# Ten of 22 small moves issued by ScalarE, a four-column marker product, and a new order of all steps in an RWKV-6 + hard-swish kernel

## The chip, the cores and the metric

The kernel runs on one core of a Trainium2 chip. The metric is the device time of one execution in microseconds (us); lower is better. The engines' names in the profile are PE (TensorE's products), PEld (its weight loads), DVE (VectorE), ACT (ScalarE), POOL (GpSimd) and SP (SyncE, which issues transfers). A `q` behind a name (SPq, ACTq) means the engine's sequencer: an instruction that only waits or issues.

## What is computed

A linear-attention recurrence over 4 batches, 8 heads, 768 positions and head size 48, and then a two-layer network with a hard-swish between its layers:

```python
for t in range(S):
    kt, vt, rt, wt = (k[:, :, t], v[:, :, t], r[:, :, t], w[:, :, t])
    cur = np.einsum('bhd,bhe->bhde', u[None] * kt, vt)
    y[:, :, t] = np.einsum('bhd,bhde->bhe', rt, state + cur)
    state = wt[:, :, :, None] * state + np.einsum('bhd,bhe->bhde', kt, vt)
...
x = y.transpose(0, 2, 1, 3).reshape(B * S, H * D)          # 3072 x 384
h = x @ w_in                                               # w_in 384 x 2048
g = h * np.clip(h + 3.0, 0.0, 6.0) / 6.0
out = g @ w_out                                            # w_out 2048 x 384
```

`w_in` and `w_out` arrive as float64 and are converted to float32 on the chip (steps `low`, `sign`, `shift`, `full`).

## The kernel before

The 768 positions of a batch are cut into chunks of 128 positions, so there are 24 chunks (numbered `i`; the two sequences of a pair alternate). Four chunks make a block of 512 rows of x; there are six blocks (`bk` 0 to 5).

Per chunk, the recurrence is a chain of small steps: two scans of the decay (`back`, `fore` on VectorE, L430 and L439), scaled keys and receptances (`K`, `R`, on VectorE for the first seven chunks and then on GpSimd, L450 and L454), the bonus term with `u` (`own`, `sum`, `diag`), scores, a masked copy (`above`, VectorE, L507), transposed keys (`turned`, ScalarE), the running state (`decay`, `mid`, `decb`, `state`), and on TensorE one step `read{i}`. From chunk 4 on `read{i}` holds, in this order, the products with the state (L578), a mark, the scores of the next chunk (L500), a mark, the key-value products of the next chunk (L600), the products with the values (L587), and the transposes of the keys of the chunk after the next (L516). A mark (L622) is a product of two corners of the identity into a scratch tile that nothing reads. Reads work on quarters of the array, so two or four products run at once.

ScalarE then copies the result into x (`leave{i}`, L685). The eight heads lie in three groups of 128 rows of x; the last pair of heads does not fit and is written to a fourth group (`x3`), from which small transfers within the chip's memory bring its rows to their places in the other three. These are the moves: `move{bk}.{p}.{g}` for pair `p` of chunks and half `g`, three transfers each (`last_pair`, L692, 16 KB a transfer). Block 0 has two moves, blocks 1 to 5 four each: 22 moves, 66 transfers. SP issues all of them.

Block 0 is multiplied plainly (`up0.f.c`, L718; `down0.c.q`, L737). Blocks 1 to 5 use a scheme with fewer products and more sums. VectorE forms sums of the weights once (`sin`, `sout`, L780 to L812) and sums of x in four steps per block (`tx{bk}.0` to `.3`, also L780 to L784), which need all four moves of the block. TensorE then forms 20 products in each of two halves (`up{bk}.{d}.{r}`, L833, four records of 256 columns each), in chains that share a bank of the product memory; `read{bk}.{d}.a{n}` take the chains' values out, on VectorE (L850) or ScalarE (L841, L848); `clip` (ScalarE, L854) and `gate` (VectorE, L858) form the hard-swish. Seven products per half follow for the second layer (`down{bk}.{p}.{k}.{x}`, L888, eight records of 192 columns), with sums of g (`sum{bk}.{p}.{k}.{x}`, VectorE, L873) and results taken out by `out{bk}.{p}.s1`, `.v`, `.u`, `.c11` and so on (ScalarE L899 and L906, VectorE L908). `vet` steps (L936, L943) check the range of the inputs on VectorE.

The order of all 1750 steps is written out: each step is added to a plan with its engine, a reckoned duration, what it needs and which buffers it takes; the string `ORDER` holds two characters per step, its rank. The steps are issued in this order, each into the queue of its engine, and each engine works its queue strictly from the front. The reckoned durations decide only two things on the chip: which of a ring's buffers a step takes follows from the order, and how many filling products TensorE gets in the first 60 us:

```python
if engine == "PE" and self.start[n] < self.UPTO:
    while now < self.start[n] - 0.12:
        self.spin()
        now += next(us_ for upto, us_ in self.SPIN if now < upto)
    now = max(now, self.start[n]) + us
```

with `SPIN = ((6.3, 0.43), (1e9, 0.224))`. A filling product (`spin`, L1269) writes a scratch bank.

Of the kernel before, what the change touches and what calls it, by code (L numbers as in the profile page):

```python
# [8 lines left out]
F32 = mybir.dt.float32  # L9
# [11 lines left out]
L = 128  # L21
# [60 lines left out]
    "AAADAHAQAKAOAMANAPARASAYAWAjAUAXAaAeAmAqAgAoAzA3A/ACAFATAiAbAnAdAZAcAfAhAlAuAyAkApAxA1A5A9A8A+BOBUBeAJALBGBfBRBZBSBD"  # L82
    "BJBTBVBYCGCLBoBwCBCRBbCYCfCnCwC7AVAwBiB4BuCABzBdBgBlBmBqCSCaCJCOCWCrCNCuC1E1DBDMDVDfBPBQCpC3DdDkCvCUCbCiDDDXDuDyC+DG"
    "DiFCDLFGFKFcFZFnCXDKC9DHEPEbDCDADQDWDsEKFgDZDqFmE6FsFvF+FzF/HgHLCcC4D+EJFpFtEDDYDwD9FfFlF8FkGFF9GVGfGiGlGsDoGSETFjGD"
    "GJEXEEFJFRF6GLG0GBGoGbGvG4HBG+HHHSHVEdF2FwF7GpG1FyGHGIGWGtGzHYGqHPG9HUHcH2HtH4FxG5F1GUGwHEHaGrGQGYHQHjH5HIINHkITIYIw"
    "I4JHL3KhGOHJGRHCHlH0H6HZGkHXH+IOJIIDKPJzK/LELJLbHKKIHOHoIqJCJEIPHmH8KxKyLOKzLKKtLXLeLmL8MHMIHbLTHhJTJeLVLdJZIJIbLULa"
    "LxLgLsL0MNL9MtJLJfJOJtLRLqLzKOJ4LFLuL+MQLtMaNANnOYOeQBOqK3L2LCLiL1MFMJLrLMMBMDMiOkNhObM/OzO4PJPVPgLfOpL4MAMyOZOsMnM9"
    "NIO1PFPeOcPiPBPmPoQJPyP2QTQZM5PcM6NdOrPbPfNpNQOCPkPrP+PlQNPsQPQUQWQcQxNtOlNuPXPqP9QAPhO5PIQIQOQlP1QsQqRSRVR/R2TPTzUG"
    "OwQjOxPxQVQrQuP0PSQRQwRySGRBSSRdSsS2ThTsUJQkTZQ+Q2RRSFSvQ/RURmS5TOT0TQTwToT1UDUPUMUQUoUTRbSQRcSLTnT8UBS7RtSNT5UKUhT9"
    "UXUEUZUkU/U2WYSATySCTqTvUSUjTrTaTuUnU0U6UmVaUlVrXGXfXnXsYIYETYURTxUOUpVOVzUWUyU+XQXmXwVMXpVyXuXzX3YAVQVRVUVeWHXqXvVh"  # L90
# [154 lines left out]
def fast_path(tc, feat, tok, wflat, ub, ug, moe_w_in, moe_w_out, out, flag, n_chunks):  # L245
# [22 lines left out]
    with ExitStack() as ctx:  # L268
# [352 lines left out]
        def mark():  # L621
            nc.tensor.matmul(pp.tile([HL, HL], F32, name="ps"), lhsT=ident[HL:, HL:], rhs=ident[HL:, HL:], start=True, stop=True)  # L622
# [378 lines left out]
        for i in range(NT):  # L1001
# [12 lines left out]
            plan.add(f"back{i}", "DVE", 1.40, do(back_scan, i), [f"feat{i}"] + [f"fore{i - 2}"] * (i > 1) + [f"back{i - 1}"] * (i > 0), k,  # L1014
                     [("E", [f"K{i}", f"least{i}"])], port=True)
            plan.add(f"K{i}", "DVE" if dve else "POOL", 0.59 if dve else 1.15, do(make_k, i), [f"back{i}", f"least{i}"] + [f"K{i - 1}"] * (i > 0) + ["later"] * (i == 0),
# [3 lines left out]
            plan.add(f"R{i}", "DVE" if dve else "POOL", 0.6 if dve else 1.15, do(make_r, i), [f"fore{i}"], k + 0.3,  # L1020
# [7 lines left out]
            else:  # L1028
                plan.add(f"own{i}", "POOL", 2.2, do(own, i), [f"rkt{i}", "u"] + [f"own{i - 1}"] * (i > 0), k + 0.4,
# [20 lines left out]
            if not first:  # L1050
                plan.add(f"decay{i}", "DVE" if dve else "POOL", 0.27 if dve else 0.9, do(decay, i),
                         [f"state{i - 2}", f"least{i}"] + [f"decay{i - 1}"] * (not is_first(i - 1)), t - 0.1 if i < len(START) else t - 5, S_, port=True)
                plan.add(f"mid{i}", "DVE", 0.33, do(middle, i), [f"kvs{i}", f"decay{i}"], t - 0.1 if i < len(START) else t - 5,
                         port=True)
            plan.add(f"decb{i}", "DVE" if dve else "POOL", 0.27 if dve else 0.9, do(decay_middle, i),
                     [f"least{i}"] + [f"mid{i}" if not first else f"kvs{i}"], t - 0.1 if i < len(START) else t - 5, S_ * first,
                     port=True)
            if not last:
                plan.add(f"state{i}", "DVE", 0.27, do(new_state, i), [f"decb{i}"] + [f"decay{j}" for j in (i - 2,) if j >= 0 and not is_first(j)],
                         t + 0.5, port=True)  # L1060
# [15 lines left out]
            else:  # L1076
                uses = [f"up{bk}.{d}.{r}" for d in range(2) for r in range(20) if X_PLACE[r][0] == "w"] + [f"tx{bk}.{x}" for x in range(4)]
                space = [("x", uses)] * (c == 0)
                needs, us = [f"decb{i}", f"above{i}"], 1.24
# [538 lines left out]
```

## Time and profile before

| | us |
|---|---|
| three runs | 540.81, 542.64, 541.25 |
| median | 541.25 |
| the profiled execution's own time | 542.08 |
| its span, first to last instruction | 540.2 |
| TensorE busy in the span | 530.0 |
| VectorE busy | 416.6 |
| ScalarE busy | 263.5 |
| GpSimd busy | 110.2 |
| granted TensorE clock, mean | 1.00 |

The own time is what the chip reports for the execution that was profiled; 1.88 us of it lie outside the span. Products on TensorE are pipelined: a record is longer than the distance to the next one, so "busy" counts a short wait only in part.

### The profile page before, as it was taken

The page shows a single profiled execution, that of the slowest core. Times are in us where ns is not written, and L with a number is a line of the kernel's source. Part 1 is how long each engine was busy: PE and PEld are TensorE (multiplying, and loading weights), DVE is VectorE, ACT ScalarE, POOL GpSimd, SP SyncE. Part 2 cuts the span into 40 slices and gives each one's busy share as a digit, 9 for nine tenths or more (in the row PEclk, how much of TensorE's full clock was granted, in tenths as well). Part 3 has the DMA queues.
Part 4 walks back from the last instruction along what each step waited for, and adds up shares of the span by engine and source line. Part 5 has one row for each costly group of instructions (what it writes and reads, how often), then busy time and mean ns, then how long its engine had stood idle before and what let it go on. Part 6 is the DMA issues. An engine that isn't in the chain of part 4 may idle for free. (4 is left out here: it accounts for less than half of the span.)

```text
span 540.2 us, 13522 instructions
## 1 busy us (share of the span) xinstructions
PE 530.0 (98%) x5626; PEld 470.1 (87%) x5626; DVE 416.6 (77%) x709; ACT 263.5 (49%) x657; POOL 110.2 (20%) x111
## 2 busy tenths in 40 slices
PE   8999999999999999999999999999999999999997
PEld 8887877666788999888889988899988999988997
DVE  8999999675999996889787888967768845358651
ACT  5999795252555434446434354635254435253400
POOL 2000003742422054111332341303350001000000
PEclk9999999999999999999999999999999999999999
DMA  8948653333234434733205785002630001100001
GB/s 341 368 160 312 237 177 105 116 106 105 74 115 151 139 94 164 250 133 130 95 17 193 256 282 205 1 10 92 208 134 1 0 2 36 41 1 1 8 8 47
DMA packets 21458, 66.42 MB, mean 123 GB/s; under 512 B 3312, under 2 KB 11408, under 8 KB 21392
## 3 DMA queue, kind: packets, MB, share of 16 engines
q1 hardware_dynamic: 21264, 65.50, 35.3%
q8 instruction: 46, 0.75, 0.5%
q14 instruction: 20, 0.16, 0.1%
q10 hardware_dynamic: 128, 0.00, 0.0%
HBM read 59.69 MB, written 4.72 MB: 119 GB/s over the span
## 5 line engine op out<-in xcount | busy, mean ns | idle before, releaser
L854 ACT ACTIVATE clip<-g,three 128x512 f32<-128x512 f32 x80 | 56.3, 720 | 55.0 <-DVE g L850 38.9
L850 DVE TENSOR_TENSOR g<-bank,g 128x512 f32<-128x512 f32 x80 | 53.4, 681 | 16.0 <-PE bank L833 15.1
L858 DVE SCALAR_TENSOR_TENSOR g<-clip,g 128x512 f32<-128x512 f32 x80 | 57.9, 740 | 6.1 <-ACT clip L854 5.9
L888 PE MATMUL bank<-w_out,g 128*128 128x192 f32 x320 | 57.3, 328 | 1.0 <-DVE g L858 1.0
L888 PEld LDWEIGHTS bank<-w_out,g 128*128 128x128 f32 x320 | 52.5, 190 | 2.5 <-DVE g L858 1.5
L491 ACT ACTIVATE A<-eyes,dg 128x64 f32<-128x64 f32 x192 | 50.4, 339 | 6.6 <-PE y_ps L587 6.3
L450 POOL TENSOR_TENSOR K<-feat_in,E 112x512 f32<-112x512 f32 x17 | 24.4, 1433 | 121.4 <-PE ps L622 117.7
L454 POOL TENSOR_TENSOR W<-feat_in,W 112x512 f32<-112x512 f32 x17 | 22.3, 1312 | 116.7 <-DVE W L439 108.9
L718 PE MATMUL bank<-xT,w_in 128*128 128x256 f32 (+1 forms) x216 | 45.2, 361 | 0.0
L685 ACT COPY xT<-y_ps 48x256 f32<-48x256 f32 x88 | 32.1, 365 | 24.8 <-PE y_ps L587 23.9
L737 PE MATMUL bank<-w_out,g 128*128 128x384 f32 x128 | 43.2, 488 | 0.0
L833 PE MATMUL bank<-xT,w_in 128*128 128x256 f32 x160 | 40.9, 381 | 0.8 <-DVE g L850 0.7
L718 PEld LDWEIGHTS bank<-xT,w_in 128*128 128x128 f32 x216 | 36.7, 190 | 4.7
L848 ACT COPY g<-bank 128x512 f32<-128x512 f32 x50 | 28.9, 582 | 21.5 <-PE bank L833 21.3
L737 PEld LDWEIGHTS bank<-w_out,g 128*128 128x128 f32 x128 | 23.8, 190 | 14.5
L439 DVE TENSOR_TENSOR_SCAN W<-feat_in,start 112x520 f32<-112x520 f32 x24 | 29.6, 1234 | 8.6 <-PE y_ps L578 8.6
L833 PEld LDWEIGHTS bank<-xT,w_in 128*128 128x128 f32 x160 | 30.0, 190 | 5.9 <-DVE g L850 2.1
L430 DVE TENSOR_TENSOR_SCAN E<-feat_in,back 112x520 f32<-112x520 f32 x24 | 32.5, 1354 | 2.9 <-DMA feat_in<-in_feat_dram 1.3
L841 ACT ACTIVATE bankS<-bank 128x512 f32<-128x512 f32 x20 | 11.6, 582 | 40.4 <-PE bank L833 31.9
L833 PE MATMUL bank<-xT,bits 128*128 128x256 f32 x120 | 30.7, 381 | 0.0
L888 PE MATMUL bankS<-w_out,g 128*128 128x192 f32 x160 | 28.8, 326 | 0.0
L888 PE MATMUL bank<-more,g 128*128 128x192 f32 x160 | 28.1, 326 | 0.0
(291 smaller groups left out, 1136.7 us busy)
## 6 DMA issues: line engine op xcount, KB each, us to landing
feat_in<-in_feat_dram SPq DMA_DIRECT2D x23, 772.5 KB, 4.8
bits<-in_moe_w_in_dram SPq DMA_DIRECT2D x8, 768.0 KB, 5.4
bits<-in_moe_w_out_dram SPq DMA_DIRECT2D x8, 768.0 KB, 5.7
feat_in<-in_moe_w_in_dram SPq DMA_DIRECT2D x8, 768.0 KB, 4.8
feat_in<-in_moe_w_out_dram SPq DMA_DIRECT2D x8, 768.0 KB, 4.6
rk_in<-in_tok_dram SPq DMA_DIRECT2D x15, 384.0 KB, 5.1
v_in<-in_tok_dram SPq DMA_DIRECT2D x24, 192.0 KB, 4.5
feat_in<-in_wflat_dram SPq DMA_DIRECT2D x6, 768.0 KB, 4.6
```

What stands on the lines that cost most here:

```text
L430: nc.vector.tensor_tensor_scan(out=E_[:, ::-1], data0=d["w"][:, :0:-1], data1=back.rearrange("q p t -> q (p t)")[:, ::-1], initial=0.0, op ...
L439: nc.vector.tensor_tensor_scan(out=W_, data0=d["w"][:, :-1], data1=starts[i % 2].rearrange("q p t -> q (p t)"), initial=0.0, op0=ALU.mult, ...
L491: nc.scalar.activation(out=d["A"][:, h, :], in_=eyes, func=ACT.Copy, scale=d["dg"][:, h])
L685: nc.scalar.copy(out=blocks[bk]["xT"][g * GP:g * GP + D, :, at:at + HL], in_=st[i]["y_ps"][a][(g ^ a) * GP:(g ^ a) * GP + D, :, :])
L718: nc.tensor.matmul(h_ps[:, :(c1 - c0) * L], lhsT=w_in[:, f // 2, j, f % 2, :], rhs=b["xT"][:, j, c0 * L:c1 * L], start=(j == 0), stop=(j = ...
L737: nc.tensor.matmul(b["o", c][:, :DM], lhsT=g_of(0, f, c), rhs=w_out[:, f, :], start=(f == 0), stop=(f == NFC - 1))
L833: nc.tensor.matmul(b["p", d, c][:, z * HB:(z + 1) * HB], lhsT=weight(W_PLACE[r], d)[:, z, :], rhs=x_at(bk, X_PLACE[r]), start=fresh and z ...
L848: nc.scalar.copy(out=out_, in_=src)
L850: nc.vector.tensor_tensor(out=out_, in0=src, in1=out_of(bk, d, other), op=ALU.add if sign > 0 else ALU.subtract)
L854: nc.scalar.activation(out=c, in_=out_of(bk, d, u), func=ACT.Relu, bias=three, scale=twice)
L858: nc.vector.scalar_tensor_tensor(out=g, in0=blocks[bk]["r", d, u], scalar=6.0, in1=g, op0=ALU.min, op1=ALU.mult)
L888: nc.tensor.matmul(b["d", p, to][:, :h], lhsT=a, rhs=w(), start=(f == 0 and k in (1, 5)), stop=(f == HF - 1 and k in (2, 3, 4)), skip_grou ...
```

## The change

Three edits, and prices of steps that the order was searched with.

*Moves.* Of each block from 1 on, the two moves with `g` = 1 are put into ScalarE's queue and issued from there; those with `g` = 0, and both of block 0, stay with SP. That is ten moves, 30 transfers.

```diff
-                    plan.add(f"move{bk}.{c // 2}.{g}", "SP", 1.8, do(last_pair, bk, c - 1, c + 1, g, nc.sync),
+                    plan.add(f"move{bk}.{c // 2}.{g}", "ACT" if g and bk else "SP", 1.8, do(last_pair, bk, c - 1, c + 1, g, nc.scalar if g and bk else nc.sync),
                              [f"leave{i - 1}", f"leave{i}"], when(i) - 50, kb=1, dmas=3)
```

*Marks.* The product of a mark streams 4 columns instead of 64; its weights are the same 64 x 64.

```diff
-            nc.tensor.matmul(pp.tile([HL, HL], F32, name="ps"), lhsT=ident[HL:, HL:], rhs=ident[HL:, HL:], start=True, stop=True)
+            nc.tensor.matmul(pp.tile([HL, 4], F32, name="ps"), lhsT=ident[HL:, HL:], rhs=ident[HL:, :4], start=True, stop=True)
```

*Order.* The string `ORDER` is replaced. It was searched with a plan in which transfers land in the order of their issue; that search is not part of the kernel. The reckoned durations that went with it change in the kernel too:

```diff
-  back 1.40, K 1.15 and R 1.15 and own 2.2 and decay 0.9 and decb 0.9 on POOL, mid 0.33, state 0.27, read 1.24
+  back 1.44, K 1.27 and R 1.22 and own 2.45 and decay 0.75 and decb 0.7 on POOL, mid 0.36, state 0.35, read 1.31
-  gate of block 0: 0.07 + 0.134 m; sin 0.34; sout 0.86; tx 0.335 per sum; gate 0.6; sum of g 0.61
+  gate of block 0: 0.08 + 0.136 m; sin 0.39; sout 0.92; tx 0.46 per sum; gate 0.62; sum of g 0.64
```

(The last block is the list of the values, not the source's lines.) Decoded from the two strings, these are the pieces of the queues that the prediction speaks of:

```
TensorE before: ... down0.2.3 read7 down0.2.4 .. down0.3.5 read8 down0.3.6 up1.0.1 down0.3.7 up1.0.9 up1.0.3 ...
TensorE after:  ... down0.2.1 read7 down0.2.2 .. down0.3.1 read8 down0.3.2 .3 .4 up1.0.1 down0.3.5 .6 .7 up1.0.18 up1.0.14 up1.0.9 ...
VectorE before: ... above8 sin1.2 sin1.3 back11 sin1.4 tx1.0 sin1.5 tx1.1 sin1.6 fore10 sin1.7 state8 sin1.8 above9 ...
VectorE after:  ... above8 sin1.2 sum10 sin1.3 sout2.1 sin1.4 above9 sin1.5 tx1.0 sin1.6 tx1.1 sin1.7 tx1.2 sin1.8 tx1.3 ...
ScalarE after:  ... leave7 diag18 least10 diag09 turned9 move1.0.1 diag19 move1.1.1 drain0.2 read1.0.a4 drain0.3 ...
ScalarE after, blocks 2, 4: ... out1.0.s1 out1.0.v move2.0.1 out1.0.u ...; ... out3.0.v move4.0.1 least20 out3.0.u ... out3.1.v kvs20 least22 move4.1.1 ...
ScalarE after, block 5: ... leave22 out4.0.c11 move5.0.1 leave23 out4.0.v out4.0.u move5.1.1 ...
SP before:      ... feat11 move1.0.1 rkt11 move1.1.0 move1.1.1 feat12 move1.0.0 rkt12 ...
SP after:       ... feat11 move1.0.0 store0.0 rkt10 rkt11 move1.1.0 feat12 tok10 rkt12 ...
POOL before:    K7 K8 R7 own9 decay7 own10 K9 R8 decb7 decay8 R9 decb8 decay9 K10 ...
POOL after:     K7 decay7 K8 R7 own9 decb7 R8 K9 decay8 decb8 K10 own10 R9 ...
VectorE before, block 2: ... gate2.1.0 sum2.0.1.1 sum2.0.2.0 sum2.0.2.1 sum17 state14 sum2.0.4.0 sum2.0.3.1 sum2.0.4.1 ...
VectorE after,  block 2: ... gate2.1.0 sum2.0.2.0 sum2.0.3.0 mid14 sum16 sum2.0.1.1 vet10.0 sum2.0.2.1 sum2.0.3.1 sum2.0.4.0 sum2.0.4.1 ...
TensorE before, block 4: read19 down3.1.6.1 3.0.2.0 3.1.7.0 3.0.2.1 3.1.3.0 3.1.7.1 3.1.3.1 3.1.4.0 read20 up4.0.1 ...
TensorE after,  block 4: read19 down3.1.6.0 3.1.6.1 3.1.3.0 3.1.3.1 3.1.7.0 3.1.7.1 read20 up4.0.1 ...
```

More of the change, by code (lines that the diff above doesn't have):

```diff
@@ L86 @@
[L86 to L90, printed above, removed]
@@ L1013, in fast_path @@
                          hold=[("rk_in", [f"own{i}"])])
-            plan.add(f"back{i}", "DVE", 1.40, do(back_scan, i), [f"feat{i}"] + [f"fore{i - 2}"] * (i > 1) + [f"back{i - 1}"] * (i > 0), k,
+            plan.add(f"back{i}", "DVE", 1.44, do(back_scan, i), [f"feat{i}"] + [f"fore{i - 2}"] * (i > 1) + [f"back{i - 1}"] * (i > 0), k,
                      [("E", [f"K{i}", f"least{i}"])], port=True)
-            plan.add(f"K{i}", "DVE" if dve else "POOL", 0.59 if dve else 1.15, do(make_k, i), [f"back{i}", f"least{i}"] + [f"K{i - 1}"] * (i > 0) + ["later"] * (i == 0),
+            plan.add(f"K{i}", "DVE" if dve else "POOL", 0.59 if dve else 1.27, do(make_k, i), [f"back{i}", f"least{i}"] + [f"K{i - 1}"] * (i > 0) + ["later"] * (i == 0),
                      k + 0.1, [("K", [scored(i), turned_by(i)])], port=True)
@@ L1019, in fast_path @@
                      [("W", [scored(i), read_by(i)])], port=True)
-            plan.add(f"R{i}", "DVE" if dve else "POOL", 0.6 if dve else 1.15, do(make_r, i), [f"fore{i}"], k + 0.3,
+            plan.add(f"R{i}", "DVE" if dve else "POOL", 0.6 if dve else 1.22, do(make_r, i), [f"fore{i}"], k + 0.3,
                      port=True)
@@ L1028, in fast_path @@
             else:
-                plan.add(f"own{i}", "POOL", 2.2, do(own, i), [f"rkt{i}", "u"] + [f"own{i - 1}"] * (i > 0), k + 0.4,
+                plan.add(f"own{i}", "POOL", 2.45, do(own, i), [f"rkt{i}", "u"] + [f"own{i - 1}"] * (i > 0), k + 0.4,
                          [("rk", [f"sum{i}"])], port=True)
@@ L1050, in fast_path @@
             if not first:
[L1051 removed]
+                plan.add(f"decay{i}", "DVE" if dve else "POOL", 0.27 if dve else 0.75, do(decay, i),
                          [f"state{i - 2}", f"least{i}"] + [f"decay{i - 1}"] * (not is_first(i - 1)), t - 0.1 if i < len(START) else t - 5, S_, port=True)
[L1053 removed]
+                plan.add(f"mid{i}", "DVE", 0.36, do(middle, i), [f"kvs{i}", f"decay{i}"], t - 0.1 if i < len(START) else t - 5,
                          port=True)
[L1055 removed]
+            plan.add(f"decb{i}", "DVE" if dve else "POOL", 0.27 if dve else 0.7, do(decay_middle, i),
                      [f"least{i}"] + [f"mid{i}" if not first else f"kvs{i}"], t - 0.1 if i < len(START) else t - 5, S_ * first,
@@ L1058, in fast_path @@
             if not last:
-                plan.add(f"state{i}", "DVE", 0.27, do(new_state, i), [f"decb{i}"] + [f"decay{j}" for j in (i - 2,) if j >= 0 and not is_first(j)],
+                plan.add(f"state{i}", "DVE", 0.35, do(new_state, i), [f"decb{i}"] + [f"decay{j}" for j in (i - 2,) if j >= 0 and not is_first(j)],
                          t + 0.5, port=True)
@@ L1078, in fast_path @@
                 space = [("x", uses)] * (c == 0)
-                needs, us = [f"decb{i}", f"above{i}"], 1.24
+                needs, us = [f"decb{i}", f"above{i}"], 1.31
                 if i + 1 < NT:
@@ L1120, in fast_path @@
                 plan.add(f"ramp{n_}", "ACT", 0.1 + 0.135 * m, do(ramp, f, c0, c1), [f"up{n_}"], k - 3, [("clip", [f"gate{n_}"])])
-                plan.add(f"gate{n_}", "DVE", 0.07 + 0.134 * m, do(gate, f, c0, c1),
+                plan.add(f"gate{n_}", "DVE", 0.08 + 0.136 * m, do(gate, f, c0, c1),
                          [f"ramp{n_}"] + [f"gate0.{f // HF * HF}.0"] * (f % HF > 0 or c0 > 0), k - 3,
@@ L1149, in fast_path @@
                     before += all_up
-                plan.add(f"sin{d}.{w_}", "DVE", 0.34, do(sum_w, w_, d), before, SUMS[0] + (w_ + 21 * d) * SUMS[1], hold, port=True)
+                plan.add(f"sin{d}.{w_}", "DVE", 0.39, do(sum_w, w_, d), before, SUMS[0] + (w_ + 21 * d) * SUMS[1], hold, port=True)
         for n_, (t_, x) in enumerate((t_, x) for t_ in (1, 2, 4, 3) for x in range(2)):
@@ L1156, in fast_path @@
                 before += [f"{ready}{len(pairs) - 1}"]
-            plan.add(f"sout{t_}.{x}", "DVE", 0.86, do(sum_out, t_, x), before, SUMS[2] + n_ * SUMS[1],
+            plan.add(f"sout{t_}.{x}", "DVE", 0.92, do(sum_out, t_, x), before, SUMS[2] + n_ * SUMS[1],
                      [("bits", ["end"])] * (t_ == 1 and x == 0) + [("top", ["end"])] * (t_ == 2) + [("more", ["end"])] * (t_ == 4),
@@ L1166, in fast_path @@
             for x in range(4 * (bk > 0)):
-                plan.add(f"tx{bk}.{x}", "DVE", 0.335 * (X_PARTS[x + 1] - X_PARTS[x]), do(sum_x, bk, x),
+                plan.add(f"tx{bk}.{x}", "DVE", 0.46 * (X_PARTS[x + 1] - X_PARTS[x]), do(sum_x, bk, x),
                          moves + [f"leave{bk * BC + c}" for c in range(BC)] + [f"tx{bk}.{x - 1}"] * (x > 0), K + TX + x,
@@ L1213, in fast_path @@
                              [("clip", [f"gate{bk}.{d}.{x}"])])
-                    plan.add(f"gate{bk}.{d}.{x}", "DVE", 0.6, do(up_gate, bk, d, x), [f"clip{bk}.{d}.{x}"], at + 0.866 * due[FINAL[x]] + GATE,
+                    plan.add(f"gate{bk}.{d}.{x}", "DVE", 0.62, do(up_gate, bk, d, x), [f"clip{bk}.{d}.{x}"], at + 0.866 * due[FINAL[x]] + GATE,
                              port=True)
```

65 lines of the change are left out of this document (35 added, 30 removed).

## The prediction

> **What bounds the kernel now.** I read the page's busy lines first, then the wait list of TensorE, then busy time by stretch, then single stretches of the timeline.
>
> ```profile
> PE 530.0 (98%) x5626; PEld 470.1 (87%) x5626; DVE 416.6 (77%) x709; ACT 263.5 (49%) x657; POOL 110.2 (20%) x111
> PE bank L833 <- DVE g L850: 1.4, 3, 0.7
> PE bank L833 <- DVE A L507: 1.2, 1, 1.2
> PE bank L888 <- DVE g L858: 1.0, 1, 1.0
> PE bank L888 <- ACT o L906: 0.4, 1, 0.4
> PE bank L888 <- DVE S__2970 L873: 0.4, 1, 0.4
> PE bank L888 <- DVE S__2285 L873: 0.2, 1, 0.2
> ```
>
> TensorE is busy for 98% of the span, and from 60 to 500 us it stands still in only eight places, 4.6 us together. No engine but TensorE can bound the whole; a gain can come only from these places, from shorter TensorE work, or from the two ends. A standstill costs more than its idle time, because a product's record runs on while the next should have started:
>
> ```profile
> 262.24 1.46 PE L888 MATMUL bank<-w_out,g 128*128 128x192 f32 x8
> 264.72 1.57 PE L888 MATMUL bank<-w_out,g 128*128 128x192 f32 x8 [1.02 <-DVE g L858]
> 266.13 1.14 PE L888 MATMUL bankS<-w_out,g 128*128 128x192 f32 x6
> ...
> 507.15 1.30 PE bank L888 x8
> ```
>
> In the undisturbed chain eight such products take 1.30. Here 2.48 passes before the next eight start (1.18 lost, of it 1.02 idle), and these take 1.41 (0.11 more). So a place costs its idle time and about 0.27, and the eight cost 4.6 + 8 x 0.27 = 6.8 us. That is all an order can win. Where they lie, by stretch:
>
> ```profile
> core 0: us, PE busy (x) PEld busy (x) DVE busy (x) ACT busy (x) POOL busy (x), PEclk, DMA share, GB/s
> 115.00:136.00 21.00, 20.28 (x231) 13.03 (x222) 12.71 (x26) 8.29 (x26) 6.84 (x7) 1.00 0.43 133
> 136.00:160.00 24.00, 23.40 (x213) 19.66 (x214) 23.90 (x45) 11.93 (x26) 7.54 (x7) 1.00 0.25 75
> 160.00:182.00 22.00, 21.38 (x108) 18.90 (x107) 21.97 (x30) 12.05 (x25) 4.94 (x4) 1.00 0.49 158
> 235.00:260.00 25.00, 24.27 (x221) 20.53 (x220) 24.31 (x38) 15.40 (x29) 5.06 (x4) 1.00 0.28 94
> 260.00:276.00 16.00, 14.19 (x84) 13.34 (x83) 11.62 (x14) 4.85 (x15) 6.45 (x6) 1.00 0.24 77
> ```
>
> VectorE is full from 136 to 182 and nearly so from 235 to 260, and TensorE waits for it there; just before, from 115 to 136, VectorE is idle for 8.3 of 21 us. The granted clock is 1.00 throughout. Why it was idle:
>
> ```profile
> 129.37 0.43 DVE L780 SCALAR_TENSOR_TENSOR T__1817<-xT 128x256 f32<-128x256 f32 x1 [5.00 <-DMA rk_in<-in_tok_dram]
> 135.96 0.76 DVE L507 COPY_PREDICATED A<-mask,bank 128x256 f32<-128x256 uint8 x2
> 115.67 1.51 ACT L685 COPY xT<-y_ps 48x256 f32<-48x256 f32 x4 [4.21 <-PE y_ps L587]
> 117.11 1.78 SPq L692 DMA_DIRECT2D xT<-xT  x3
> 119.56 4.11 SPq L692 DMA_DIRECT2D xT<-xT  x6
> 124.34 1.77 SPq L692 DMA_DIRECT2D xT<-xT  x3
> L692 SPq DMA_DIRECT2D xT<-xT x66: 507/582/1447, 50.0 to 459.8; - x66
> DMA to landing us min/median/max: 1.7/3.3/4.9
> ```
>
> The step `tx1.0` (L780) needs all four moves of block 1. The leave that the last two need ends at 117.18, but SP issues the four one after the other between loads, until 126.11; about 3.3 later `tx1.0` starts, after 5.00 of waiting. The row names another transfer, yet `tx1.0` reads only x. Behind it in VectorE's queue stands `above9` (135.96), for which the first product of chain 5, `up1.0.9`, waits 1.2. So one late move costs a place at once, and 5.0 us of VectorE's time that are missing in the full stretch behind.
>
> **The change part by part.**
>
> *Moves on ScalarE.* Ten of the 22 moves, three transfers each, go from SP to ScalarE: 30 x 0.582 = 17.5 us of issue join its 263.5 busy us of 540. The halves of a pair are then issued side by side, which ends the series 1.8 earlier per pair, and they no longer stand behind the loads of SP's queue. SP's queue for block 1 is now `feat11`, `move1.0.0`, `store0.0`, `rkt10`, `rkt11`, `move1.1.0`, `feat12`; on POOL `R8`, which frees the slot of `feat11`, stands ahead of `own10` and `K9`, where it stood behind both. What stands behind a move on ScalarE: in block 1 `diag19`, `drain0.2` and `read1.0.a4`; in blocks 2 and 4 `out.u`, for which product 7 waits. There `out.v` can run after product 5, the move takes 1.8, and product 6 takes 2 x 1.30 = 2.6 before `out.u` could start: covered. At block 5 `leave23` stands behind `move5.0.1`, and `move5.1.1` behind `out4.0.u`. Cost 0 where covered; the tightest place is the start of block 4:
>
> ```profile
> 373.56 1.50 ACT L685 COPY xT<-y_ps 48x256 f32<-48x256 f32 x4 [3.17 <-PE y_ps L587]
> 373.89 1.48 PE L888 MATMUL bank<-top,S__4134 128*128 128x192 f32 x8
> 384.40 0.67 PE L578 MATMUL y_ps<-W,S 48*48 48x64 f32 x32
> 387.04 1.04 PE L833 MATMUL bank<-T__4366,bits 128*128 128x256 f32 x4
> 383.35 0.41 DVE L780 SCALAR_TENSOR_TENSOR T__4366<-xT 128x256 f32<-128x256 f32 x1
> ```
>
> Now eight groups of 1.30 and `read20` (2.64) lie between `read19` and `up4.0.1`, 13.1 us; the new order leaves six, 10.4 us. The chain to be hidden: `leave19` ends 1.2 after `read19`; `out3.1.v`, `kvs20` and `least22` on ScalarE 1.0; issue 1.75; landing 3.3; `tx4.0` 1.8 (its four sums follow each other at about 0.45): 9.1. Spare 1.3. With the longest landing, 4.9, and the longest issue, 3 x 1.447 = 4.3, it is 13.2 and a hole of 2.8. Zero is taken, because the median rows fit; the other end is kept for the range.
>
> *Marks.* 38 marks, two records each, keep their 64x64 weights and stream 4 columns in place of 64.
>
> ```profile
> L622 PE MATMUL ps<-ident 64*64 64x64 f32 x76 | 10.5, 217 | 0.0
> L475 PE MATMUL ps<-u_col,rk 112*64 112x2 f32 x144 | 5.7, 200 | 0.3 <-DVE rk L463 0.3
> 77.79 0.63 PE L475 MATMUL ps<-u_col,rk 112*64 112x2 f32 x16
> 13.86 0.65 PE L578 MATMUL y_ps<-W,S 48*48 48x64 f32 x16
> ```
>
> The nearest rows: 16 products with 2 columns take 0.63, 16 with 64 columns 0.65, both two at a time on parts of the array. Columns hardly set their pace, so loading the weights must. Bound: the records differ by 17 ns, and 76 x 17 = 1.3 us; a loss is excluded, since nothing is added. The L475 rows are nearest: 0 is taken, 0 to -1.3 kept.
>
> *The order.* Decoded, all five queues are unchanged up to `up0.13.2`, about 73 us. After it `read4` to `read8` come two to four products earlier, `above9` stands ahead of `tx1.0`, the 42 weight sums stand ahead of fewer reads, and in block 2 `sum2.0.3.1` and `vet10.0` fill VectorE while product 5 runs. The prices alter nothing on the chip but the number of filling products (L1269, the rule in `emit`), which is 36 for 34; at the 0.224 us that the code reckons each, 0 to 0.45; 0.3 is taken, as one of the two stands where TensorE may have been waiting anyway. Place by place:
> - `up1.0.9`, 1.2 + 0.27 = 1.5: goes, `above9` no longer stands behind the moves.
> - Block 1's other two (0.2 of L873 and about 0.4 of the 1.4 of L850, with 2 x 0.27): 1.2 go, as VectorE gets the 5.0 us back.
> - The end of block 2 (0.4 + 0.4 + 0.54 = 1.35): goes. Product 3 waited there for `out2.0.u` and `sum2.0.4`, and two sums that took 1.48 to 1.49 beside POOL's work:
>
> ```profile
> 271.57 1.49 DVE L873 TENSOR_TENSOR S__2970<-g,S__2970 128x512 f32<-128x512 f32 x1
> 272.98 1.48 DVE L873 TENSOR_TENSOR g<-g 128x512 f32<-128x512 f32 x1
> ```
>
> In the new order `sum2.0.3.1` comes before product 6, and only `sum2.0.4.0` and its second half are left at 0.6 to 0.7 each.
> - The other three (1.0 + 0.27, and two of L850 with 1.0 + 0.54): 2.8 in all. VectorE's work ahead of them changes by under 1.5, and POOL's still falls beside it; half, 1.4, goes.
> - What is late next: eight places in five blocks says that such an order leaves one or two per block on the chip; reads that come earlier make one new place of the mean size, 6.8/8 = 0.9; 1.0 is charged, 0 to 6.8 kept.
>
> Sum: -1.5 - 1.2 - 1.35 - 1.4 + 0.3 + 1.0 = -4.15. The span goes from 540.2 to 536.05, and this execution's own 542.08 (1.88 lie around its span) to 537.9. The median of the three runs, 541.25, is 0.8 lower, and there it is 537.1.
>
> **The rivals.**
> 1. *The holes move.* VectorE's work is the same, and a stretch with 23.90 busy of 24 can't be emptied by order alone. For it: three of five stretches are full. Against it: 8.3 idle us lie just ahead of two of them. All 6.8 stay, +0.3: 541.5, no change.
> 2. *The moves land no sooner.* With large loads on the way a move may take what it took before, whichever queue issued it. Then block 1's 2.7 stay: 541.25 - 4.15 + 2.7 = 539.8, no measurable change. For it: landing varied from 1.7 to 4.9 on one queue. Against it: most of the lateness was SP's series from 117.1 to 126.1, and that is shorter whatever the transfers do. The Trainium skill, "DMA: Bandwidth & Descriptors", section "Issuing engines are not separate DMA queues", says this: transfers started by several engines interleave on the same 16 DMA engines, and only the time to issue them is saved. No run here shows yet a move from ScalarE.
> 3. *The moves come too late, slower.* ScalarE reaches a move only after its own steps, and each block's first products have `tx` before them. It decides when issue and landing pass 5.05 + 1.3 = 6.3 us at block 4. With the 2.8 hole at all five starts 14 would be lost; half, 7, is the price, since blocks 1 to 3 have nine products or more between read and start. 541.25 - 4.15 + 7 = 544.1.
> 4. *All goes.* No place left, and the marks give their 1.3: 541.25 - 6.8 - 1.3 + 0.3 = 533.5. Against it: the full stretches and the L475 rows.
>
> **How the numbers follow.** Forecast 0.56, rival 1 0.13, rival 2 0.09, rival 3 0.15, rival 4 0.07. A measurement tells about 0.3% (1.6 us) from no change. Faster: forecast and rival 4, 0.63; same: rivals 1 and 2, 0.22; slower: rival 3, 0.15. The forecast's own range is 535 to 539.5. The whole one reaches from rival 4 down at 533.5, past rivals 1 and 2 with the same spread, to 543.5, and leaves out most of rival 3 and half of rival 4.
>
> **What would show it.** Right: no idle time of TensorE before the first products of chain 5 in block 1; VectorE's idle time before `tx1.0` well under 5.0; the waits of TensorE between 60 and 500 us at 1 to 2.5 us in place of 4.6; the moves at L692 on two queues at about 0.58 per transfer, landing in 3.3 or less; L622 at about 200 ns with the reads as long as before (2.64 from first product to the next). Wrong: new rows among TensorE's waits that name L780, L784 or a transfer of x; ScalarE's `out` steps late behind moves; VectorE full in stretches that were not.

## The result, and the profile after

| | before | after |
|---|---|---|
| median of ten runs each, us | 542.02 | 539.00 |
| lowest and highest | 540.81, 543.98 | 538.34, 540.66 |
| ratio, 95% interval | | 0.9947 (0.9934 to 0.9960) |
| the profiled execution's own time | 542.08 | 539.36 |
| its span | 540.2 | 537.6 |

The change makes the kernel 0.5% faster, 2.9 us by the ratio. From the page of the changed kernel, the busy lines and the line of its DMA part for TensorE's code (packets, MB, share), used further down; then TensorE's waits between 60 and 500 us (total, times, longest):

```profile
PE 529.7 (99%) x5630; PEld 471.8 (88%) x5630; DVE 414.1 (77%) x709; ACT 264.1 (49%) x657; POOL 110.6 (21%) x111
...
q8 instruction: 46, 0.75, 0.6%
```

```profile
PE y_ps L587 <- issue: 1.3, 1, 1.3
PE bank L833 <- DVE g L850: 0.5, 1, 0.5
PE bank L888 <- DVE S__2965 L873: 0.5, 1, 0.5
PE bank L888 <- DVE S__4063 L873: 0.3, 1, 0.3
PE bank L833 <- ACT bankS L841: 0.2, 1, 0.2
```

Eight places with 4.6 us of idle time have become five with 2.8. Only the second, third and fifth are of the old kind and in the old stretches. The first is new and names no engine ("issue"). By stretch, with the columns of the table before:

```profile
115.00:136.00 21.00, 21.00 (x195) 13.41 (x194) 17.28 (x31) 5.78 (x19) 8.04 (x7) 1.00 0.22 74
136.00:160.00 24.00, 23.35 (x214) 19.58 (x213) 21.99 (x40) 14.45 (x35) 7.57 (x8) 1.00 0.34 98
160.00:182.00 22.00, 21.97 (x113) 19.63 (x113) 21.90 (x33) 13.60 (x31) 5.21 (x5) 1.00 0.39 129
235.00:260.00 25.00, 25.00 (x231) 22.44 (x230) 23.24 (x38) 16.81 (x36) 2.13 (x2) 1.00 0.43 146
260.00:276.00 16.00, 15.50 (x212) 14.71 (x211) 12.24 (x19) 4.34 (x16) 6.92 (x7) 1.00 0.31 103
```

VectorE works 17.28 us of the first stretch (12.71 before), yet it is still nearly full from 136 to 182. TensorE is now busy throughout 235 to 260 and lacks 0.50 from 260 to 276, where 1.81 was lacking.

The waits in the list count idle time alone. Measured from one product's start to the next, less the ordinary distance of such products, the places behind 60 us cost 8.1 us before and 4.9 after. That is 3.2 won; 1.0 of it was given back at the start (below). The end of the last product comes 2.4 earlier, so 0.2 more is spread over places too small to name.

The moves and the marks (count, then duration in ns min/median/max):

```profile
L692 SPq DMA_DIRECT2D xT<-xT x36: 507/582/1360, 50.8 to 455.5; - x36
L692 ACTq DMA_DIRECT2D xT<-xT x30: 514/600/771, 117.5 to 457.2; - x30
DMA to landing us min/median/max: 1.7/2.4/6.5
L622 PE MATMUL ps<-ident x76: 167/182/196, 80.1 to 448.0; 64*64 64x4 f32 x76
```

A mark is recorded at 182 ns in place of 217, but a read takes 2.64 us as before.

### The profile page after: what moved, and what is told of

Its sections match the earlier page's. It is cut to its first block, busy times and chain, and to the rows that moved or that the text cites. A ratio compares the mean times of both kernels' runs of the same rounds, so it can differ in the third digit from the quotient of the medians.

```text
span 537.6 us, 13516 instructions
## 1 busy us (share of the span) xinstructions
PE 529.7 (99%) x5630; PEld 471.8 (88%) x5630; DVE 414.1 (77%) x709; ACT 264.1 (49%) x657; POOL 110.6 (21%) x111
## 4 chain that ended last, share of the span: by engine, by line
PE 95%; DVE 3%; ACT 1%; issue 1%; POOL 0%; POOLq 0%; ACTq 0%
PE bank L888 29%; PE bank L833 26%; PE bank L737 8%; PE bank L718 7%; PE bankS L888 5%; PE bankS L833 5%; PE y_ps L578 2%; PE y_ps L587 2%; PE bankS L1269 2%; PE bank L500 2%; PE ps L516 2%; PE y_ps L600 2%; PE ps L475 1%; DVE g L858 0%; DVE g L850 0%
## 5 line engine op out<-in xcount | busy, mean ns | idle before, releaser
L850 DVE TENSOR_TENSOR g<-bank,g 128x512 f32<-128x512 f32 x80 | 53.6, 684 | 23.1 <-PE bank L833 19.7
L858 DVE SCALAR_TENSOR_TENSOR g<-clip,g 128x512 f32<-128x512 f32 x80 | 55.9, 716 | 7.8 <-ACT clip L854 7.6
L430 DVE TENSOR_TENSOR_SCAN E<-feat_in,back 112x520 f32<-112x520 f32 x24 | 30.1, 1255 | 1.3 <-DMA feat_in<-in_feat_dram 1.3
L906 ACT ACTIVATE o<-bank 128x192 f32<-128x192 f32 x30 | 9.7, 329 | 40.5 <-PE bank L888 40.5
L466 POOL TENSOR_TENSOR rk<-rk_in 128x384 f32<-128x384 f32 x15 | 20.5, 1364 | 39.1 <-DVE dg L483 23.7
```

Source lines behind the costliest of these rows:

```text
L430: nc.vector.tensor_tensor_scan(out=E_[:, ::-1], data0=d["w"][:, :0:-1], data1=back.rearrange("q p t -> q (p t)")[:, ::-1], initial=0.0, op ...
L850: nc.vector.tensor_tensor(out=out_, in0=src, in1=out_of(bk, d, other), op=ALU.add if sign > 0 else ALU.subtract)
L858: nc.vector.scalar_tensor_tensor(out=g, in0=blocks[bk]["r", d, u], scalar=6.0, in1=g, op0=ALU.min, op1=ALU.mult)
```

## The experiments

Each ratio is to the kernel before, run on the same chip, with its 95% interval.

**The changed kernel again, for a second profile.** No edit.

> The changed kernel once more. In its first profile TensorE stands still for 1.3 us in the middle of the value products of read20 (L587), and no semaphore ends it. Theory A: this is code that TensorE waits for (the 16 KB packet of its instruction queue that starts at 380.2), it belongs to the program, and it stands at the same place again with 1.0 to 1.6 us; ratio 0.993 to 0.997. Theory B: an accident of that one execution; then TensorE's waits between 60 and 500 us add up to about 1.5 us, not 2.8, and the place is empty. The start: with the filling products before dot0 as many as before, dot0 starts anywhere from 7.2 to 7.9 us, wherever the step of the filling products falls from 0.21 to 0.11 us.

0.9955 (0.9938 to 0.9972), 539.05 us. TensorE's row around `read20` in the first profile of the changed kernel, then in this one:

```profile
379.17 0.67 PE L578 MATMUL y_ps<-W,S 48*48 48x64 f32 x32
...
380.77 0.56 PE L587 MATMUL y_ps<-A,v_in 64*48 64x64 f32 x23
382.66 0.31 PE L587 MATMUL y_ps<-A,v_in 64*48 64x64 f32 x3 [1.34 <-issue]
```

```profile
380.08 0.67 PE L578 MATMUL y_ps<-W,S 48*48 48x64 f32 x32
...
382.29 0.60 PE L516 MATMUL ps<-ident,K 112*128 112x112 f32 x4
```

The same code runs through here without a stop. But this execution waits longer for L850, twice and 1.3 us in all, where the other waited once for 0.5:

```profile
PE bank L833 <- DVE g L850: 1.3, 2, 0.8
```

 So places come and go between executions of one kernel, and one profile alone doesn't tell what a place costs.

**The new order alone.** All moves on SyncE, marks of 64 columns.

```diff
- "ACT" if g and bk else "SP"      - rhs=ident[HL:, :4]
+ "SP"                             + rhs=ident[HL:, HL:]
```

> The new order with all moves on SP and marks of 64 columns. If the order carries the gain (above9 ahead of tx1.0, sums earlier): ratio 0.995 to 0.997, with the pairs of moves one after the other on SP (1.8 us later each) costing at most 1 us at blocks 4 and 5. If the moves on ScalarE carry it: ratio 0.999 to 1.001, with VectorE waiting several us at tx1.0 and new standstills at the block starts.

0.9950 (0.9933 to 0.9967), 539.15 us: all of the gain, as far as the intervals tell. Its moves, issued by SyncE alone, land as soon as the changed kernel's (median 2.4):

```profile
L692 SPq DMA_DIRECT2D xT<-xT x66: 507/587/1719, 50.9 to 458.3; - x66
DMA to landing us min/median/max: 1.7/2.3/6.0
```

In block 1 they even land sooner. SyncE issues the nine transfers of its last three moves one behind the other, and `tx1.0` finds them there and waits for nothing. First two rows of this kernel's timeline, then four of the changed kernel's (by engine: ScalarE's issues, SyncE's load, VectorE):

```profile
115.81 5.57 SPq L692 DMA_DIRECT2D xT<-xT  x9
...
127.38 0.42 DVE L780 SCALAR_TENSOR_TENSOR T__1886<-xT 128x256 f32<-128x256 f32 x1
```

```profile
120.10 0.60 ACTq L692 DMA_DIRECT2D xT<-xT  x1
125.49 0.52 ACTq L692 DMA_DIRECT2D xT<-xT  x1
121.30 0.33 SPq L352 DMA_DIRECT2D feat_in<-in_feat_dram  x1
129.12 0.43 DVE L780 SCALAR_TENSOR_TENSOR T__1886<-xT 128x256 f32<-128x256 f32 x1 [1.80 <-issue]
```

On ScalarE the last transfer of `move1.1.1` stands 4.8 us behind the one ahead of it. In the trace each transfer waits for, and then raises, one of eight semaphores that go round in the program's order. This one had been given to the load at L352, which SyncE issues at 121.30 and which lands at 125.47; the move is issued at 125.49 and lands at 129.04. Before the change the last transfer landed at 129.25. So in block 1 ScalarE gives back what the new order had won for the moves. It costs TensorE no place there, whether `above9` stands ahead of `tx1.0`, as here, or behind it (`above_behind`, below).

**The moves on ScalarE in the old order.** The move line of the change and nothing else.

> The old order with the ten moves on ScalarE, marks of 64 columns. If the issue alone matters: tx1.0 waits about 3 us instead of 5.0 (move1.0.0 still stands on SP behind feat12), up1.0.9 waits 1.2 less or not at all, ratio 0.996 to 0.998. If the order is needed to use it: ratio 0.999 to 1.001. If ScalarE's 17.5 us of issue hurt: above 1.002.

1.0039 (1.0022 to 1.0056), 543.75 us: slower. TensorE's waits, and the place in block 4 on ScalarE and TensorE:

```profile
PE bank L833 <- DVE A L507: 1.4, 1, 1.4
PE bank L888 <- ACT o L906: 1.3, 3, 0.7
```

```profile
375.64 1.79 ACTq L692 DMA_DIRECT2D xT<-xT  x3
377.48 0.33 ACT L906 ACTIVATE o<-bank 128x192 f32<-128x192 f32 x1 [1.87 <-issue]
377.87 1.57 PE L888 MATMUL bank<-w_out,g 128*128 128x192 f32 x8 [0.66 <-ACT o L906]
```

Block 1's place is gone here, as the moves land early enough for `tx1.0` to start at 127.43. But an `out` step stands behind a move's three issues, TensorE waits for it (three such waits, 1.3 us; the old order had one of 0.4), and a new place of 1.4 opens at the start of block 2. This is rival 3 of the prediction, in the old order.

**The marks alone.** Old order, old moves, 4 columns.

> The old order, moves on SP, only the marks with 4 columns. By the prediction nothing: the reads take 2.64 us as before, since the weight load sets the pace; ratio 0.999 to 1.001. The rival (the records get shorter by 17 ns, 76 of them on the path): 1.3 us, 0.9976, reads 2.57 us.

1.0011 (1.0001 to 1.0022), 542.07 us. Reads still take 2.64 us. Fewer columns buy nothing.

**`above9` put behind `tx1.1` again.** The changed kernel; `above9` is moved from ahead of `sin1.5` to directly behind `tx1.1`.

> The changed kernel with one step moved: above9 stands behind tx1.0 and tx1.1 again, as in the old order. By the prediction's first place above9 is then held up for as long as tx1.0 waits and takes, and the first products of chain 5 in block 1 (up1.0.14, up1.0.9) stand still: TensorE's waits show 0.5 to 1.5 us more that name L507, and the time is 0.5 to 1.5 us above the changed kernel's. Rival: with the moves of block 1 issued earlier tx1.0 no longer waits, so the place stays empty either way, and the time is the changed kernel's (539.0).

0.9950 (0.9935 to 0.9965), 539.14 us: as the changed kernel. VectorE waits 4.81 us before `tx1.0`, as long as before the change, and still no place opens at `up1.0.9`. One row of TensorE in the kernel before, then two of TensorE and one of VectorE in this kernel:

```profile
136.44 1.13 PE L833 MATMUL bank<-T__1817,w_in 128*128 128x256 f32 x4 [1.16 <-DVE A L507]
```

```profile
132.01 4.03 PE L737 MATMUL bank<-w_out,g 128*128 128x384 f32 x12
...
136.74 1.89 PE L833 MATMUL bank<-T__1884,w_in 128*128 128x256 f32 x8
129.12 0.43 DVE L780 SCALAR_TENSOR_TENSOR T__1884<-xT 128x256 f32<-128x256 f32 x1 [4.81 <-issue]
```

In the old order one product of the second layer lies between `up1.0.1` and `up1.0.9`. In the new one three lie there, and `up1.0.18` and `up1.0.14`, so that `up1.0.9`, the second half of the row at 136.74, starts at about 137.6. `above9` itself runs from 132.31 to 133.08 here. The old kernel had it done only at 136.72, since there `fore10` and `state8` stand ahead of it too. So in the new order the place stays empty without `above9` ahead of `tx1.0` and without early moves. In the old order early moves alone emptied it (`before_act`, where `up1.0.9` starts at 135.57 without a wait). That TensorE's new order alone would do it, with `above9` as late as 136.72, was not tried; with its start at 137.6 it should.

**Where in the order the gain lies.** Four seams, all with old moves and old marks. `new_then_old`: the steps that the old order has ahead of `tx2.0` (783 of 1750), in the new sequence, and the old order behind. `old_then_new`: the steps that the new order has ahead of `tx2.0`, in the old sequence, and the new order behind. `new_block2`: the old order up to `tx2.0`, the new one from there to `tx3.0`, the old one behind. `new_last`: the new order only from `tx3.0` on.

```diff
- ORDER = old
+ new_then_old: new 1..tx2.0 | old        old_then_new: old 1..tx2.0 | new
+ new_block2:   old | new tx2.0..tx3.0 | old    new_last: old 1..tx3.0 | new
```

> The old kernel (moves on SP, marks of 64) with the new order for the 783 steps that stood ahead of tx2.0, block 1's, and the old order behind. If block 1 is where the gain is, as the prediction's first two terms say (2.7 of 4.15): ratio about 0.995, and TensorE's waits up to 182 us fall from 2.0 to under 0.5. By the places seen in the changed kernel (1.5 us left there of 3.25): ratio 0.996 to 0.998.

> The counterpart: old order up to tx2.0, new order behind it; moves on SP, marks of 64. By the prediction (1.35 and half of 2.8, less 1.0 of new places): 1.7 us, ratio 0.997. By the places seen in the changed kernel (4.8 us after 200 us before, 1.4 to 3.4 after): ratio 0.994 to 0.997. The two halves together should give the 0.995 of the whole order.

`new_then_old` 0.9994 (0.9978 to 1.0010), 541.18 us. `old_then_new` 0.9944 (0.9925 to 0.9962), 539.06 us. Block 1 in the new order takes the places there from 3.3 to 1.5 us, but the time stays: a new place opens at the start of block 2:

```profile
219.38 1.13 PE L833 MATMUL bank<-T__2742,bits 128*128 128x256 f32 x4 [1.15 <-DVE A L507]
```

 Neither whole order has this place. In this kernel GpSimd works beside the sums of `tx2.0` (from 214.30 to 218.23 us), and the first three sums take 1.19, 1.11 and 0.61 us. They take 0.41, 0.62 and 0.43 in the kernel before and 0.44, 0.42 and 0.42 in the changed one. So the place belongs to the seam, and this run doesn't show that block 1's new order is worth nothing: with the place taken off, at 1.15 + 0.27 us, it would stand at 0.997, which was not run. What the pair shows is that the order behind `tx2.0` brings as much as the whole order without block 1's.

> The old kernel with the old order up to step tx2.0, the new order from there to tx3.0, the old one behind. All moves on SyncE, marks of 64 columns. The new order behind tx2.0 gave 0.9944. Theory A (the gain is block 2's, where the places at 236.6 to 274.4 us summed to 4.1 us in the old kernel and to 1.0 in the changed one): 0.9945, about 539.1 us, those places gone, the one at 346 us (0.73 in the old kernel) still there. Theory B (the gain lies in the last two blocks, in work that stands in no hole): 0.999 to 1.000, 541.5 us or more.

> The old kernel with the old order up to step tx3.0, the new order behind. All moves on SyncE, marks of 64 columns. Theory A (the gain is block 2's): 0.999 to 1.000, with block 2's places of 236.6 to 274.4 us unchanged, 4.1 us in sum. Theory B (the gain lies in the last two blocks): 0.9945 to 0.996. If both share it, this one and the other seam lie between, and the two gains add up to about 0.0056.

`new_block2` 0.9983 (0.9969 to 0.9998), 541.21 us; `new_last` 0.9994 (0.9978 to 1.0009), 542.26 us. Both theories miss: the two gains make 0.0023, not 0.0056. `new_last` has block 2's old places, but for one at 237.7 us, and rules out that the blocks behind it carry the gain by themselves. `new_block2` has lost block 2's old places but has one at its start, which `old_then_new` has not. `new_block2` first (TensorE, VectorE, GpSimd), then `old_then_new` in the same sequence:

```profile
220.34 1.13 PE L833 MATMUL bank<-T__2748,bits 128*128 128x256 f32 x4 [1.53 <-DVE o L908]
215.99 1.57 DVE L780 SCALAR_TENSOR_TENSOR T__2748<-xT,T__2748 128x256 f32<-128x256 f32 x1
217.60 1.10 DVE L782 TENSOR_TENSOR T__2748<-T__2748,xT 128x256 f32<-128x256 f32 x1
218.74 1.28 DVE L780 SCALAR_TENSOR_TENSOR T__2748<-xT,T__2748 128x256 f32<-128x256 f32 x1
216.29 0.99 POOL L466 TENSOR_TENSOR rk<-rk_in 128x384 f32<-128x384 f32 x1
```

```profile
219.15 1.03 PE L833 MATMUL bank<-T__2734,bits 128*128 128x256 f32 x4
216.50 0.62 DVE L780 SCALAR_TENSOR_TENSOR T__2734<-xT,T__2734 128x256 f32<-128x256 f32 x1
217.15 0.42 DVE L782 TENSOR_TENSOR T__2734<-T__2734,xT 128x256 f32<-128x256 f32 x1
217.61 0.43 DVE L780 SCALAR_TENSOR_TENSOR T__2734<-xT,T__2734 128x256 f32<-128x256 f32 x1
218.57 1.00 POOL L466 TENSOR_TENSOR rk<-rk_in 128x384 f32<-128x384 f32 x1 [1.75 <-DVE dg L483]
```

The prefixes of the two differ by eight steps. One of them is `sum14` on VectorE (L483), which GpSimd's next products (L466) need. In `new_block2` it comes ahead of `tx2.0`, so GpSimd works beside the sums of `tx2.0`, and three of these take 1.57, 1.10 and 1.28 us. In `old_then_new` it comes behind them; GpSimd waits 1.75 us for it, and the sums take 0.62, 0.42 and 0.43. That is 2.5 us of VectorE's time, and 1.53 of idle time on TensorE. The place of `sum14` is only half of the reason: the kernel before has it ahead of `tx2.0` too, and there the same sums take 0.62, 0.43 and 0.42. There GpSimd has `K15` and `own15` ahead of `decay14` and is done with both at 216.65, before the first sum. In `new_block2` it has `decay14` first, which waits 3.00 us for `state12`, and `own15` and `K15` fall beside the sums. So this place, too, is one of the seam, and neither whole order has it. The Trainium skill, "SBUF — State Buffer", section "Who interferes with whom", says that a VectorE instruction with two inputs in SBUF contends with a GpSimd instruction that reads SBUF. These rows agree with it.

With that place, at 1.53 + 0.27 us or 0.33%, taken off, `new_block2` would stand at 0.995. So the gain is mostly block 2's; this last step is argued and was not run. The profile is of the fastest of the twelve runs (539.70, median 541.21), so how often the place stands there isn't known.

**Fewer filling products.** Of the changed kernel's 36, the four first ones and thirteen more stay, nineteen go, with fixed numbers in place of the rule:

```diff
-                while now < self.start[n] - 0.12:
-                    self.spin() ...
+                for _ in range(self.SPINS.get(n, 0)):
+                    self.spin()
+    SPINS = {"dot0": 9, "turn0": 1, "read0": 1, "read1": 2}
```

> The changed kernel with 17 filling products in place of 36: four at the start and 9 before dot0, 1 before turn0, 1 before read0, 2 before read1, none elsewhere. In its profile read1 starts as the last of six filling products ends, while what it reads (third1) was there 0.8 us before, and dot3 and read3 each start 0.22 later for one. Theory: a filling product that TensorE had no time for stands in the path; up to up0.13.2 1.0 to 2.5 us are won, 0.991 to 0.993 against the kernel before. Rival: with less to do TensorE's step stays at 0.21 us for longer or falls back to it, and the start is as long as before or longer: 0.995 or above.

0.9960 (0.9927 to 0.9994), 538.6 us, but in two groups: seven runs between 536.85 and 538.6, five between 543.7 and 550.27. The ratio mixes them. The profile is of the first group (span 535.6). The second was not profiled, but the mean granted clock of every run is on record: 0.996 to 1.000 in the first group, 0.991 in the three runs of 543.70 to 544.20, 0.978 in the two of 549.38 and 550.27. The traces know only two values of the clock, 1.0 and 0.5. By these, an estimate, the second group spent about 10 and 24 us at half the clock, which costs about 5 and 12 us; these runs are some 6 and 12 longer. So the theory holds in the first group (its median, 537.85, is 0.992 of the kernel before), and the rival came true in the second: with so few filling products the clock fell back in five of twelve runs. Where in the execution it did isn't shown.

Then only the eight behind `read0` left out:

```diff
+    SPINS = {"dot0": 12, "turn0": 3, "kv0": 1, "clear0": 1, "turn1": 2, "first0": 2, "read0": 3}
```

> The changed kernel with its own filling products up to read0, and none behind: the 6 before read1, the 1 before dot3 and the 1 before read3 are left out (8 of 32). Theory A (these stand in the path, and TensorE's step, which is 0.11 us a product by then, stays there): 8 products and their share of the queue go, 0.8 to 1.5 us, ratio to before 0.992 to 0.9935, all runs within 1 us of each other. Theory B (they fill waits that are there anyway): 0.995, the wait of TensorE before read1 longer by what they took. Theory C (the runs that were 5 to 13 us longer when 17 of them had gone come back): two groups again, one above 543 us, so that even the late ones hold the step down.

0.9934 (0.9911 to 0.9956), 538.83 us, all six runs between 537.03 and 539.17 and each with a granted clock of 1.0. Theory C falls; these eight don't hold the clock. The first of the 76 weight loads of marks stands in the row's "first and last" column, in the second run of the changed kernel and then here; the first products at L475 start at 7.17 and 7.10:

```profile
L622 PEld LDWEIGHTS ps<-ident x76: 131/134/136, 79.7 to 447.3; 64*64 64x64 f32 x76
```

```profile
L621 PEld LDWEIGHTS ps<-ident x76: 131/134/135, 78.1 to 445.6; 64*64 64x64 f32 x76
```

So the eight stand in the path and cost 1.6 us in these profiles. In the runs the interval reaches from 0.9911 to 0.9956 and overlaps that of the changed kernel: it beats the kernel before, and whether it beats the changed one stays open.

**TensorE's code moved.** Sixteen small products in place of three of the first four filling ones:

```diff
-            for _ in range(4): spin()
+            spin()
+            for k in range(16): nc.tensor.matmul(still[0:32, 0:32], lhsT=ident[0:32, 0:32], rhs=ident[0:32, 0:32], ...)
```

> The changed kernel with three of its four first filling products replaced by 16 products of 32 rows and 32 columns, which lie at the start before the first transfer lands, so that TensorE's code behind them lies 13 instructions later. Theory A (the wait inside read20's value products in the changed kernel's profile, 1.55 us at 381.1 us, is TensorE waiting for its next 16 KB of code): no such wait there, or another size of it; if there is one, it stands in another place of the same stretch or in another run of short products. Theory B (it comes from the order of the work at that place): it stands inside read20's value products again with 1.0 us or more. Time 0.994 to 0.997 by either.

0.9970 (0.9954 to 0.9986), 540.72 us. `read20` runs without a stop, 2.20 us from its first product to the transposes (2.21 in the second profile of the changed kernel):

```profile
383.23 0.67 PE L579 MATMUL y_ps<-W,S 48*48 48x64 f32 x32
...
385.43 0.60 PE L517 MATMUL ps<-ident,K 112*128 112x112 f32 x4
```

The queue q8 fetches 46 packets of 16 KB, 0.75 MB, or one for each 245 of TensorE's 11,260 products and loads. By the packets' times in the traces, the fetch near `read20` starts 1.05 us behind the read's start in the changed kernel's first profile, and TensorE goes on 2.44 us after it starts; with the order alone it goes on 2.36 us after. In the second profile the fetch starts 0.43 ahead of the read, in this kernel 1.91 ahead, and there is no stop in either. `code_shift` alone settles little, since the second profile of the unchanged code has no stop either. The traces together settle more. In twelve of them a fetch starts within 2 us of the start of `read20`. The read takes 2.64 or 2.65 us, from its first product to the next chain, where the fetch starts 0.39 us or more ahead of it; 2.98 where it starts 0.17 ahead (`above_behind`); 3.00 and 3.19 where it starts 0.55 and 0.50 behind (`new_last`, `old_then_new`); 3.71 at 0.67 (`order_only`) and 4.18 at 1.05. In each of these five stops, and in two more of `spin_cut`, TensorE goes on 2.3 to 2.5 us after the fetch starts. So theory A fits: the stop is TensorE waiting for code, and it comes when the fetch starts late against a run of short products. The start of this kernel is 1.5 us late for another reason (last section).

## Why the prediction was right, and where it was not

The forecast was 537.1 us, a gain of 4.15; the runs gave 2.9. The sign and the cause, a new order that empties places of TensorE, held: `order_only` gives all of it. That the total fell so near is partly luck: single terms missed by up to 2.1 us, in both directions. Step by step, with the cost of places from start to start in the two profiles:

- *`up1.0.9`, -1.5.* It went, 1.4. But the reason given, `above9` ahead of the moves, isn't needed: `above_behind` keeps `above9` behind `tx1.0`, and the place stays empty, as TensorE has five products between `up1.0.1` and `up1.0.9` where it had one.
- *The rest of block 1, -1.2.* This step failed. These places fell from 1.8 to 1.5 only. VectorE did use the idle time ahead, 17.28 against 12.71 busy us, but its stretches behind stayed nearly full, at 21.99 of 24 and 21.90 of 22. `new_then_old` gained nothing in time, but has a place of its own at the seam, so what block 1's order is worth stays open.
- *The end of block 2, -1.35.* Mis-sized: 1.3 became 1.0. The sums were put earlier, but one ran beside GpSimd again and took 1.67, where 0.6 to 0.7 was reckoned (VectorE, GpSimd, TensorE):

```profile
266.57 1.67 DVE L873 TENSOR_TENSOR S__2965<-S__2965,g 128x512 f32<-128x512 f32 x1 [2.42 <-PE bank L888]
266.51 1.19 POOL L450 TENSOR_TENSOR K<-feat_in,E 112x512 f32<-112x512 f32 x1
268.30 1.57 PE L888 MATMUL bank<-top,S__2965 128*128 128x192 f32 x8 [0.46 <-DVE S__2965 L873]
```

- *The other three, -1.4.* Mis-sized the other way: 3.5 stood there and all of it went. Part of that is chance: the place at 237.7 us, the longest wait for L850 with 0.7 of idle time, is missing in the four other profiles with block 2's old order (`before_act`, `before_marks4`, `new_then_old`, `new_last`). `old_then_new` has the whole gain from the order behind `tx2.0`.
- *New places, +1.0.* Came to 2.45, of which 1.6 is the wait for code at `read20`, which the prediction had not thought of and which only some executions have.
- *Filling products, +0.3.* Near: the changed kernel is 0.56 late at the first products of L475 and 1.0 late at 74 us, so 0.45 came in between. Two places with a filling product more cost 0.22 each; a third cost 0.04, and where one fewer stands, a wait of 0.2 for L417 at 40.4 us took its time. The 0.56 came on top, 7.83 for 7.27, though the number of filling products ahead is the same; in the second profile of the same kernel L475 starts at 7.17, so that part is chance.
- *Marks, 0.* Right: 182 ns recorded, reads as long as before. The Trainium skill, "TensorE: Matmul & The Clock Gate", section "LDWEIGHTS (loading the stationary operand)", lets the cost go with the weights' columns; the marks kept theirs, and `before_marks4` at 1.0011 agrees.
- *Moves on ScalarE, 0 where covered.* Right in the new order, but they won nothing either: `order_only` without them is as fast. In the new order SyncE alone lands block 1's moves earlier than the two queues do. Rival 2 came true in block 1, where the last move landed at 129.04 for 129.25, through the semaphore that it shared with a load and not through contention. Rival 3's mechanism, `out` behind a move, was seen in the old order at +0.4%.

The measures named beforehand: no idle time at `up1.0.9`, right; VectorE's wait before `tx1.0` 1.80, right; TensorE's waits 2.8 where 1 to 2.5 was given, and 2.2 in the second profile.

Open: the profiles can't say how much of each sort of place is chance, since the same order showed 0.3, 1.0 and 1.5 us at one place (about 310 us) in three profiles; which steps of block 2's order bring the gain; what block 1's order is worth; and where in the execution the clock falls back in the second group of `spin_cut`.

## What to carry to other kernels

When VectorE's sums are in the path, keep GpSimd's steps from running beside them: its own order and the small step that starts it both decide that. Look at the durations of the same instruction before blaming its amount of work. When two orders are cut and joined, look for a place at the seam that neither has, before reading the join's time as the worth of a part. Before moving transfers to another engine's queue, see whose landing each of them waits for, and which steps will stand behind it. Price an order's gain by place over two or more profiles: places of one us came and went here between executions of one kernel.

## What the runs showed of the hardware that was not expected

- *Code.* TensorE stops for its next 16 KB of code inside a run of short products, for 0.3 to 1.5 us, and goes on 2.3 to 2.5 us after the fetch starts (seven stops, in six of the fourteen traces).
- *Semaphores of transfers.* A transfer of 0.5 us issue stood 4.8 us in ScalarE's queue for a load of SyncE's that used the same semaphore; steps behind it wait too.
- *TensorE's clock at the start.* The 32 records of the first 16 filling products took 6.46 us in one execution and 5.76 in the next of the same kernel:

```profile
1.44 6.46 PE L1269 MATMUL bankS<-ident 128*128 128x128 f32 x32 [1.44 <-POOL ident masks.py:199]
```

```profile
1.43 5.76 PE L1269 MATMUL bankS<-ident 128*128 128x128 f32 x32 [1.43 <-POOL ident masks.py:199]
```

```profile
4.00 5.36 PE L1270 MATMUL bankS<-ident 128*128 128x128 f32 x24
```

The distance of two records falls from 0.213 to 0.111 us at 6.9 us in the first and at 5.4 in the second. The traces' records of the granted clock say the same: 1.0 from 6.97 and from 5.50 us on, held for 532.48 us in both; in the kernel before it is held for 535.89, which is 3.41 longer. The Trainium skill, "TensorE: Matmul & The Clock Gate", section "Part 1: The HAM clock gate (the "warmup" mystery)", has the clock released after a busy window of about 3.4 us that runs free of the kernel's start; the 3.41 agrees with that. The Trainium skill, in the same section, gives 500 ns either way for the moment of release; here the clock came between 4.55 and 6.97 us in the traces that start as these do, which is wider. In the third row, of `code_shift`, 24 records behind sixteen products on a 32 x 32 corner still average 0.22 us, up to 9.36, and the clock comes at 9.10, which is 5.1 after the first full-size product behind the small ones; in the others it comes 3.1 to 5.5 after the first product of all. So the small products seem not to have counted as work, in this one profile.
